# Linear attention before an MLP: the last k tile normalised in halves, and the sum over tokens taken ahead of the next q projection

## The chip, the cores and the metric

The kernel runs on one core of one Trainium2 chip. The metric is the time of one execution in microseconds (us), the median of three runs. The engines are PE (matmuls), DVE (vector), ACT (scalar), POOL (GpSimd) and SP (which issues DMAs here). Each works through its own list of instructions in order; semaphores tie the lists together.

## The reference

The block has two parts, each with a layer norm in front and a residual sum behind. The change touches only the first one, a linear attention with 32 heads of 16 features over 2048 tokens of 512 channels:

```python
q, k, v = split(layernorm(x) @ wqkv)
pq, pk = q @ w_phi, k @ w_phi                       # per head
phi_q = concat(softmax(pq), softmax(-pq))           # 32 features a head
phi_k = concat(softmax(pk), softmax(-pk))
kv  = einsum("bhsf,bhsd->bhfd", phi_k, v)
z   = einsum("bhsf->bhf", phi_k)                    # sum over all tokens
num = einsum("bhqf,bhfd->bhqd", phi_q, kv)
den = einsum("bhqf,bhf->bhq", phi_q, z)[..., None] + 1e-6
h = x + (num / den) @ wo
```

The second part, a token-mixing MLP with 1792 hidden units, follows on `layernorm(h)`.

## The kernel before, in words

The tokens are cut into 16 tiles of 128 (`NT = 16`). `w_phi` is folded into the q and k weights at the start, so that one projection gives the logits. Every projection of a tile is 12 matmuls of 128x512 (`mm3`, lines 68 to 70): the operands are split into a high and a low part, and three of the four products are summed for each of four chunks of channels.

For a k tile, `k_logits` takes the maximum and the minimum of each head's logits (`mx`, `mn`, lines 166 and 167) on DVE, subtracts them (`shift`, lines 160 and 164) and takes exponentials on ACT (line 186). `k_norm` then sums each head's exponentials on DVE (`sk`), inverts the sums, multiplies the tile `pk` by them on POOL (line 210) and adds it to `zacc` (lines 212 and 214). For the two last k tiles, 14 and 15, it is called with `z=False`, and the additions are written out elsewhere: that of tile 14 on POOL (line 485), that of tile 15 on DVE in two halves (line 493).

A v tile is projected by `v_proj` (`v_kv`, matmuls into `pv`); after every fourth one, `kv` multiplies four k tiles with their v tiles into `kvp`.

A q tile goes through the same logits. `q_mm` is its projection on PE, into one of two PSUM banks of the pool `ps_q` (the tile `pu`); `q_logits` returns three DVE steps (mx, mn and `shift`); `negate` forms the second half of the exponents on POOL (lines 174 and 175); `q_exp` takes the exponentials on ACT. Six q tiles (0 to 5) pass this way within the loop over the k tiles.

When the last k tile is added, a matmul of `ones` with `zacc` (line 501, two halves of 128x512, on PE) gives z in every partition, and ACT copies it to `zB` (line 502). Then follow for each q tile: `s_ez`, POOL's product of `eq` with `zB` (line 457, tile `ez`); `s_den`, five DVE steps from `ez` to the factors `w` (lines 466 to 470); `s_pq`, POOL's product of `eq` with `w` (line 473). The loop over q tiles (`it`) transposes the result on PE, multiplies it with kv and `wo`, adds x, and forms the second layer norm: `s_rstd` on POOL (line 610), `s_hn` on ACT and POOL (`hs`, line 64).

`wo_hi` and `wo_lo` split the weights `wo`, four pieces each: the high part on ACT (`woh`, line 442), the low part by subtraction on DVE (`wol`, line 445).

From line 94 to the end of this stage the order on PE, DVE, ACT and POOL is the order in which the code is written. `run` issues lists of steps; given more than one list, it takes a step of each in turn (`turns`).

Of the kernel before, what the change touches and what calls it, by code (L numbers as in the profile page):

```python
# [17 lines left out]
P = 128  # L18
S, D, H, DH, F = 2048, 512, 32, 16, 1792
NT = S // P  # L20
# [19 lines left out]
def block_kernel(ctx: ExitStack, tc: tile.TileContext, x, xT, wT, phic, wo, w1, b1, w2, b2,  # L40
                 kvmask, ident_in, out):
    nc = tc.nc
# [59 lines left out]
    zacc = wp.tile([P, NG, P], F32, name="zacc")  # L102
# [5 lines left out]
    X, XH, EQ, PK, VS, SQ, PS, W = {}, {}, {}, {}, {}, {}, {}, {}  # L108
# [23 lines left out]
    def proj(t, wh, wl, pool, name, by_part=False):  # L132
        o = pool.tile([P, D], F32, name=name, tag=name)
        if by_part:
            half, whole = [slice(0, D // 2), slice(D // 2, D)], slice(0, D)
            turn = [(0, wh, half[0]), (0, wh, half[1]), (1, wh, whole), (0, wl, half[0]), (0, wl, half[1])]
            for i, (a, w, cols) in enumerate(turn):
                for kt in range(KD):
                    nc.tensor.matmul(o[:, cols], X[t][:, a, kt, :], w[:, kt, cols], start=i == 0 and kt == 0,
                                     stop=i >= 3 and kt == KD - 1, skip_group_check=True)  # L140
            return o
        for kt in range(KD):
            mm3(o, X[t][:, 0, kt, :], X[t][:, 1, kt, :], wh[:, kt, :], wl[:, kt, :],
                kt == 0, kt == KD - 1)
        return o
# [6 lines left out]
    def logit_ops(src, e, pool):  # L152

        v = src.rearrange("p (j h d) -> p j h d", h=2, d=DH)
        ev = signs(e)
        mx = wk.tile([P, NPR, 2], F32, name="mx")
        mn = wk.tile([P, NPR, 2], F32, name="mn")

        def shift():
            nc.vector.tensor_sub(ev[:, :, 0], v, mx.unsqueeze(3).to_broadcast([P, NPR, 2, DH]))  # L160
            if pool:
                MN.append((ev, mx, mn))
            else:
                nc.vector.tensor_sub(ev[:, :, 1], mn.unsqueeze(3).to_broadcast([P, NPR, 2, DH]), v)  # L164

        return [lambda: nc.vector.tensor_reduce(mx, v, axis=AX.X, op=ALU.max),
                lambda: nc.vector.tensor_reduce(mn, v, axis=AX.X, op=ALU.min),
                shift]

    def negate():  # L170

        if MN:
            ev, mx, mn = MN.pop(0)
            nc.gpsimd.tensor_sub(mn, mn, mx)
            nc.gpsimd.tensor_sub(ev[:, :, 1], mn.unsqueeze(3).to_broadcast([P, NPR, 2, DH]), ev[:, :, 0])

    def turns(*lists):

        return [ops[i] for i in range(max(map(len, lists))) for ops in lists if i < len(ops)]

    def run(*lists):
        for op in turns(*lists):
            op()

    def exps(t, e):
        nc.scalar.activation(e, e, AF.Exp, scale=r1[:, t:t + 1])  # L186

    def heads(e):
        return e.rearrange("p g (a d) -> p (g a) d", d=DH)
# [16 lines left out]
    def k_norm(t, z=True):  # L206
        sk = wk.tile([P, 2 * H], F32, name="sk", bufs=2)
        nc.vector.reduce_sum(sk, heads(PK[t]), axis=AX.X)
        nc.vector.reciprocal(sk, sk)  # L209
        nc.gpsimd.tensor_mul(heads(PK[t]), heads(PK[t]), sk.unsqueeze(2).to_broadcast([P, 2 * H, DH]))  # L210
        if z and t == 0:
            nc.gpsimd.tensor_copy(zacc, PK[t])
        elif z:
            nc.gpsimd.tensor_add(zacc, zacc, PK[t])  # L214
# [17 lines left out]
    with tc.tile_pool(name="prep", bufs=1) as prep:  # L232
# [70 lines left out]
        with tc.manual_schedule(engines={ET.PE, ET.DVE, ET.Activation, ET.Pool}):  # L303
# [42 lines left out]
            stats_x(2)  # L346
            k3 = proj(3, wkh, wkl, ps_k, "pk_ps")
            k_norm(0)
            center(0, True)
            v_out(0, v0)  # L350
# [5 lines left out]
            fold(0, ps_q, "pu")  # L356
            fold(1, ps_q, "pu")
            k_norm(1)
            center(2, False)
            v_out(1, v1)  # L360
# [14 lines left out]
    def q_mm():  # L375
        if q["mm"] < NT:
            PS[q["mm"]] = proj(q["mm"], wqh, wql, ps_q, "pu")
            q["mm"] += 1

    def q_logits(lag):  # L380
        n = q["logits"]
        if n < min(NT, q["mm"] - lag + NT * (q["mm"] == NT)):
            EQ[n] = big.tile([P, NG, P], F32, name="eq", tag="big")
            q["logits"] += 1
            return logit_ops(PS[n], EQ[n], n >= len(Q_AT))
        return []

    def q_exp(lag):
        n = q["exp"]
        if n < min(NT, q["logits"] - len(MN) - lag):  # L390
            exps(n, EQ[n])
            q["exp"] += 1
# [8 lines left out]
    def v_kv():  # L401

        nonlocal v
        v_proj(v)
        if v % 4 == 0:
            for t in range(v - 4, v):
                kv(t)
        v += 1
# [4 lines left out]
    for t in range(3, NT - 1):  # L413
        if t + 2 < NT:
            raw = load_x(t + 2)
            load_h(t + 2)
        if t > 3:
            k_logits(t)
        if t > 3 and t not in V_NOT:
            v_kv()  # L420
        if t > 0:
            k_norm(t - 1)
        if t + 2 < NT:
            split_x(t + 2, raw)
            stats_x(t + 2)
        if t in Q_AT:
            q_mm()
            run(q_logits(0))
            q_exp(0)
            run(q_sums(1))  # L430
# [24 lines left out]
    def s_ez(t):  # L455
        EZ[t] = az.tile([P, NG, P], F32, name="ez")
        nc.gpsimd.tensor_mul(EZ[t], EQ[t], zB)  # L457

    def s_den(t):


        tz = az.tile([P, NPR, 2, 2], F32, name="tz")
        den = az.tile([P, NPR, 2], F32, name="den")
        W[t] = az.tile([P, NPR, 2, 2], F32, name="w", bufs=3)
        other = SQ[t][:, :, ::-1]
        return [lambda: nc.vector.reduce_sum(tz.rearrange("p g c h -> p (g c h)"), heads(EZ[t]), axis=AX.X),
                lambda: nc.vector.tensor_mul(tz, other, tz),
                lambda: nc.vector.reduce_sum(den, tz.rearrange("p g c h -> p g h c"), axis=AX.X),
                lambda: nc.vector.reciprocal(den, den),
                lambda: nc.vector.tensor_mul(W[t], other, den.unsqueeze(2).to_broadcast([P, NPR, 2, 2]))]  # L470

    def s_pq(t):
        nc.gpsimd.tensor_mul(heads(EQ[t]), heads(EQ[t]), W[t].rearrange("p g c h -> p (g c h)").unsqueeze(2).to_broadcast([P, 2 * H, DH]))  # L473
# [14 lines left out]
    for j in range(KD):  # L488
        wo_hi(j)
    v_kv()  # L490
    run(q_logits(0))
    for g in range(2):
        nc.vector.tensor_add(zacc[:, 4 * g:4 * g + 4, :], zacc[:, 4 * g:4 * g + 4, :], PK[NT - 1][:, 4 * g:4 * g + 4, :])
    for j in range(KD):
        wo_lo(j)
    negate()
    q_mm()
    zB = big.tile([P, NG, P], F32, name="zB", tag="big")
    for g in range(2):
        pz = ps_k.tile([P, 4, P], F32, name="pk_ps")  # L500
        nc.tensor.matmul(pz, ones, zacc[:, 4 * g:4 * g + 4, :], start=True, stop=True)
        nc.scalar.activation(zB[:, 4 * g:4 * g + 4, :], pz, AF.Identity, bias=eps2[:, 1:])  # L502
    q_exp(0)
    s_ez(0)
    s_ez(1)
    v_kv()
    run(s_den(0))
    run(q_logits(0))
    s_pq(0)
    negate()  # L510
    q_exp(0)
# [618 lines left out]
    for n, (sp, p) in enumerate(STEPS):  # L1130
        t = 2 * sp
# [131 lines left out]
```

## Time and profile before

| | |
|---|---|
| median of 3 runs | 517.39 us (517.29 to 517.85) |
| profiled execution | 516.99 us, span 515.2 us |
| PE busy | 509.3 us, 99% of the span |
| DVE, ACT, POOL busy | 445.9, 297.2, 244.6 us |
| granted PE clock | 1.00 |

The span reaches from the first to the last instruction. A row of the timeline has the start (us from the span's start), the duration, the engine, the line of the code, the operation, the output and inputs by the program's names with their sizes, and how often it stands there in a row; in square brackets stands the idle time of the engine ahead of it with what ended it. A row of the waits has who waited, for whom, the sum in us, how often, and the longest. A row of a group has the busy time and the mean duration in ns. The timeline's end of a matmul is modelled: matmuls overlap, and their starts are what counts.

### The profile page before, as it was taken

The numbers are of one execution on the slowest core, as the hardware profiler recorded it, in microseconds if no ns is written. First come the engines' busy times: TensorE is split into PE (matmuls) and PEld (weight loads), VectorE is DVE, ScalarE is ACT, GpSimd is POOL, SyncE is SP. The second block draws the span as 40 slices with busy tenths as digits, with TensorE's granted clock in tenths as the row PEclk, the third lists the DMA queues.
The fourth block names the chain that finished last, engine by engine and source line by source line (L and its number), as shares of the span: only waits on it lengthen the run. The fifth ranks groups of instructions, "written<-read, shape, count | busy, mean of one in ns | idle before, by whom it ended". The sixth has DMA issues, their size and how long they took to land.

```text
span 515.2 us, 9360 instructions
## 1 busy us (share of the span) xinstructions
PE 509.3 (99%) x3546; PEld 439.3 (85%) x3546; DVE 445.9 (87%) x765; ACT 297.2 (58%) x494; POOL 244.6 (47%) x188
## 2 busy tenths in 40 slices
PE   8999999999999999999999999999999999999997
PEld 8888888887877778777788899998888898899897
DVE  6793999986789998777796998989989899998985
ACT  6998954525245876668976643457753444444430
POOL 2579799984999999975343300000002212211220
PEclk9999999999999999999999999999999999999999
DMA  8844311000041324333322333374135688667833
GB/s 315 268 124 123 83 45 39 1 1 2 22 145 41 103 83 142 124 123 123 112 93 83 83 104 104 101 245 137 47 123 127 161 184 165 148 140 194 166 44 78
DMA packets 36300, 58.56 MB, mean 114 GB/s; under 512 B 3744, under 2 KB 19360, under 8 KB 36256
## 3 DMA queue, kind: packets, MB, share of 16 engines
q1 hardware_dynamic: 31648, 50.85, 31.5%
q0 software_dynamic: 4032, 6.42, 9.5%
q8 instruction: 28, 0.46, 0.4%
q10 hardware_dynamic: 576, 0.69, 0.4%
q14 instruction: 16, 0.13, 0.1%
HBM read 46.81 MB, written 11.14 MB: 112 GB/s over the span
## 4 chain that ended last, share of the span: by engine, by line
PE 94%; POOL 3%; ACT 1%; DVE 1%; issue 0%; POOLq 0%
PE py L1105 20%; PE pu L935 12%; PE pu L68 8%; PE pu L69 8%; PE pu L70 8%; PE py L1109 7%; PE pv L69 3%; PE pv L70 3%; PE pv L68 3%; PE pk_ps L68 3%; PE pk_ps L69 2%; PE pk_ps L70 2%; PE tn L547 2%; PE po L70 2%; PE po L69 2%; PE po L68 2%
## 5 line engine op out<-in xcount | busy, mean ns | idle before, releaser
L1181 POOL DMA_DIRECT2D out<-ot x7 | 6.2, 885 | 157.7 <-DVE ot L1177 157.7
L991 ACT ACTIVATE whi<-wraw 128x1792 fp32r<-128x1792 f32 x28 | 47.6, 1702 | 44.2 <-DVE wraw L858 26.6
L1001 DVE TENSOR_TENSOR wlo<-wraw,whi 128x1792 fp32r<-128x1792 f32 x28 | 56.6, 2020 | 4.9 <-PE py L1109 4.7
L1105 PE MATMUL py<-uf,whi 128*128 128x512 f32 x210 | 57.6, 393 | 0.0
L69 PE MATMUL pu<-hs,whi 128*128 128x512 f32 x128 | 50.3, 393 | 1.2 <-POOL hs L64 1.2
L68 PE MATMUL pu<-hs,whi 128*128 128x512 f32 x128 | 50.1, 399 | 0.0
L70 PE MATMUL pu<-hs,wlo 128*128 128x512 f32 x128 | 47.9, 390 | 0.0
L896 ACT ACTIVATE whi<-wraw 128x896 fp32r<-128x896 f32 x24 | 22.9, 955 | 31.2 <-PE pu L935 26.2
L457 POOL TENSOR_TENSOR ez<-eq,zB 128x1024 f32<-128x1024 f32 x16 | 38.3, 2396 | 4.5 <-ACT zB L502 4.5
L1105 PEld LDWEIGHTS py<-uf,whi 128*128 128x128 f32 x210 | 35.8, 189 | 4.3
L1105 PEld LDWEIGHTS py<-uf,wlo 128*128 128x128 f32 x210 | 33.1, 190 | 4.6
L935 PE MATMUL pu<-ht,whi 128*128 128x256 f32 x192 | 35.6, 283 | 0.0
L1105 PE MATMUL py<-uf,wlo 128*128 128x256 f32 x210 | 34.9, 280 | 0.0
L210 POOL TENSOR_TENSOR pk<-pk,sk 128x1024 f32<-128x1024 f32 x16 | 31.0, 1941 | 6.3 <-DVE sk L209 6.3
L64 POOL TENSOR_TENSOR hs<-hb,hs 128x512 fp32r<-128x512 f32 x16 | 22.3, 1393 | 24.4 <-ACT hs L63 24.3
L549 ACT ACTIVATE pht<-tn 128x512 f32<-128x512 f32 x32 | 17.4, 596 | 28.6 <-PE tn L547 28.4
L473 POOL TENSOR_TENSOR eq<-eq,w 128x1024 f32<-128x1024 f32 x16 | 32.2, 2013 | 0.8 <-DVE w L470 0.8
L214 POOL TENSOR_TENSOR zacc<-zacc,pk 128x1024 f32<-128x1024 f32 x13 | 31.2, 2402 | 0.6
L186 ACT ACTIVATE pk<-pk,r 128x1024 f32<-128x1024 f32 x16 | 18.3, 1146 | 21.1 <-DVE pk L164 21.1
L68 PEld LDWEIGHTS pu<-hs,whi 128*128 128x128 f32 x128 | 24.0, 188 | 7.1 <-issue 2.5
L935 PEld LDWEIGHTS pu<-ht,whi 128*128 128x128 f32 x192 | 30.0, 192 | 0.0
L69 PEld LDWEIGHTS pu<-hs,whi 128*128 128x128 f32 x128 | 24.1, 188 | 6.6 <-POOL hs L64 2.1
(208 smaller groups left out, 1606.6 us busy)
## 6 DMA issues: line engine op xcount, KB each, us to landing
wraw<-in_w SPq DMA_DIRECT2D x28, 512.0 KB, 4.2
wraw<-in_w SPq DMA_DIRECT2D x48, 256.0 KB, 2.8
xraw<-in_xT SPq DMA_DIRECT2D x16, 256.0 KB, 3.0
xh<-in_x SPq DMA_DIRECT2D x16, 256.0 KB, 2.7
h<-in_x SPq DMA_DIRECT2D x16, 256.0 KB, 2.8
out<-h SPq DMA_DIRECT2D x14, 256.0 KB, 2.7
out<-ot POOLq DMA_DIRECT2D x14, 256.0 KB, 4.9
wraw<-in_wT SPq DMA_DIRECT2D x12, 256.0 KB, 5.1
```

The lines of the kernel that those rows point to most:

```text
L68: nc.tensor.matmul(o, ah, bh, start=first, stop=False)
L69: nc.tensor.matmul(o, ah, bl, start=False, stop=False)
L70: nc.tensor.matmul(o, al, bh, start=False, stop=last)
L210: nc.gpsimd.tensor_mul(heads(PK[t]), heads(PK[t]), sk.unsqueeze(2).to_broadcast([P, 2 * H, DH]))
L214: nc.gpsimd.tensor_add(zacc, zacc, PK[t])
L457: nc.gpsimd.tensor_mul(EZ[t], EQ[t], zB)
L473: nc.gpsimd.tensor_mul(heads(EQ[t]), heads(EQ[t]), W[t].rearrange("p g c h -> p (g c h)").unsqueeze(2).to_broadcast([P, 2 * H, DH]))
L935: nc.tensor.matmul(ACC[p][bk][:, half], WS[p, i][x][:, a], hb[b][y], start=i == 0 and half == 0 and k == 0, stop=i == NT // 2 - 1 and k == ...
L991: nc.scalar.activation(WH[g], RAW[g], AF.Copy)
L1001: nc.vector.tensor_sub(wl_, RAW[g], WH[g])
L1105: nc.tensor.matmul(o, w, u, start=p == 0 and not low, stop=p == NP - 1, skip_group_check=True)
L1109: nc.tensor.matmul(bank[bk][:, half], AW[sp, p][x][:, a], UB[p, b][:, y], start=p == 0 and half == 0 and i == 0, stop=p == NP - 1 and i == ...
```

## The change

The multiplication of the last k tile by its inverted sums becomes two instructions, each for half of the columns. DVE's additions to `zacc` are issued alternately with the logits of q tile 6 instead of behind them. The matmuls with `ones` and the copies to `zB` stand ahead of the next `q_mm` (q tile 7) instead of behind it. Further on, the first of the three logit steps of q tile 7 stands ahead of `s_den(0)`, and the other two stay behind it.

```diff
         nc.vector.reciprocal(sk, sk)
-        nc.gpsimd.tensor_mul(heads(PK[t]), heads(PK[t]), sk.unsqueeze(2).to_broadcast([P, 2 * H, DH]))
+        n = 1 if z or t < NT - 1 else 2
+        for part in range(n):
+            a = slice(2 * H // n * part, 2 * H // n * (part + 1))
+            nc.gpsimd.tensor_mul(heads(PK[t])[:, a], heads(PK[t])[:, a],
+                                 sk[:, a].unsqueeze(2).to_broadcast([P, 2 * H // n, DH]))
...
     v_kv()
-    run(q_logits(0))
-    for g in range(2):
-        nc.vector.tensor_add(zacc[:, 4 * g:4 * g + 4, :], zacc[:, 4 * g:4 * g + 4, :], PK[NT - 1][:, 4 * g:4 * g + 4, :])
+    run([lambda g=g: nc.vector.tensor_add(zacc[:, 4 * g:4 * g + 4, :], zacc[:, 4 * g:4 * g + 4, :],
+                                          PK[NT - 1][:, 4 * g:4 * g + 4, :]) for g in range(2)], q_logits(0))
     for j in range(KD):
         wo_lo(j)
     negate()
-    q_mm()
     zB = big.tile([P, NG, P], F32, name="zB", tag="big")
     for g in range(2):
         pz = ps_k.tile([P, 4, P], F32, name="pk_ps")
         nc.tensor.matmul(pz, ones, zacc[:, 4 * g:4 * g + 4, :], start=True, stop=True)
         nc.scalar.activation(zB[:, 4 * g:4 * g + 4, :], pz, AF.Identity, bias=eps2[:, 1:])
+    q_mm()
     q_exp(0)
     s_ez(0)
     s_ez(1)
     v_kv()
-    run(s_den(0))
-    run(q_logits(0))
+    ops = q_logits(0)
+    run(ops[:1], s_den(0))
+    run(ops[1:])
     s_pq(0)
```

On DVE, this is the stretch from the last inverted sums of a k tile to the first factors `w`, before the change (`pu_1473` holds the logits of q tile 6, `pu_1523` those of q tile 7, `pk_1370` is k tile 15):

```order
L209 RECIPROCAL sk_1486<-sk_1486 128x64
L166 TENSOR_REDUCE mx_1510<-pu_1473 128x32
L167 TENSOR_REDUCE mn_1511<-pu_1473 128x32
L160 TENSOR_TENSOR eq_1509<-pu_1473,mx_1510 128x16x32
L493 TENSOR_TENSOR zacc_109<-zacc_109,pk_1370 128x512 x2
L445 TENSOR_TENSOR wol_1383<-wor_1384,woh_1382 128x512 x4
L466 TENSOR_REDUCE tz_1563<-ez_1544 128x64
L467 TENSOR_TENSOR tz_1563<-smq_83,tz_1563 128x64
L468 TENSOR_REDUCE den_1564<-tz_1563 128x32
L469 RECIPROCAL den_1564<-den_1564 128x32
L470 TENSOR_TENSOR w_1565<-smq_83,den_1564 128x64
L166 TENSOR_REDUCE mx_1572<-pu_1523 128x32
```

The same stretch of DVE after the change, where `pu_1531` holds the logits of q tile 7:

```order
L209 RECIPROCAL sk_1486<-sk_1486 128x64
L495 TENSOR_TENSOR zacc_109<-zacc_109,pk_1370 128x512
L166 TENSOR_REDUCE mx_1511<-pu_1473 128x32
L495 TENSOR_TENSOR zacc_109<-zacc_109,pk_1370 128x512
L167 TENSOR_REDUCE mn_1512<-pu_1473 128x32
L160 TENSOR_TENSOR eq_1510<-pu_1473,mx_1511 128x16x32
L449 TENSOR_TENSOR wol_1383<-wor_1384,woh_1382 128x512 x4
L166 TENSOR_REDUCE mx_1565<-pu_1531 128x32
L470 TENSOR_REDUCE tz_1567<-ez_1545 128x64
L471 TENSOR_TENSOR tz_1567<-smq_83,tz_1567 128x64
L472 TENSOR_REDUCE den_1568<-tz_1567 128x32
L473 RECIPROCAL den_1568<-den_1568 128x32
```

Both additions now stand ahead of mn and `shift` of q tile 6, and the maximum of q tile 7 stands between the four `wol` and `tz`. All else keeps its order; the line numbers of the second half are 2 to 4 higher.

On POOL, the rows from the addition of k tile 14 to the first two `ez` and the first `s_pq`, before the change:

```order
L485 TENSOR_TENSOR zacc_109<-zacc_109,pk_1323 128x1024
L210 TENSOR_TENSOR pk_1370<-pk_1370,sk_1486 128x1024
L174 TENSOR_TENSOR mn_1511<-mn_1511,mx_1510 128x32
L175 TENSOR_TENSOR eq_1509<-mn_1511,eq_1509 128x16x32
L457 TENSOR_TENSOR ez_1544<-eq_584,zB_1536 128x1024
L457 TENSOR_TENSOR ez_1546<-eq_779,zB_1536 128x1024
L473 TENSOR_TENSOR eq_584<-eq_584,w_1565 128x1024
```

And the same rows of POOL after it:

```order
L489 TENSOR_TENSOR zacc_109<-zacc_109,pk_1323 128x1024
L213 TENSOR_TENSOR pk_1370<-pk_1370,sk_1486 128x512 x2
L174 TENSOR_TENSOR mn_1512<-mn_1512,mx_1511 128x32
L175 TENSOR_TENSOR eq_1510<-mn_1512,eq_1510 128x16x32
L461 TENSOR_TENSOR ez_1545<-eq_584,zB_1524 128x1024
L461 TENSOR_TENSOR ez_1547<-eq_779,zB_1524 128x1024
L477 TENSOR_TENSOR eq_584<-eq_584,w_1569 128x1024
```

Only the multiplication has changed, from one instruction to two of half the width.

## The prediction

> **What bounds the kernel now.** I read the page first: busy time by engine and the chain of work that ended last.
>
> ```profile
> PE 509.3 (99%) x3546; PEld 439.3 (85%) x3546; DVE 445.9 (87%) x765; ACT 297.2 (58%) x494; POOL 244.6 (47%) x188
> PE 94%; POOL 3%; ACT 1%; DVE 1%; issue 0%; POOLq 0%
> ```
>
> PE is busy for 509.3 of 515.2 us, and the chain is PE for 94%. Work moved on another engine is worth only what it does to a moment in which PE stands still. So the second view is PE's own waits, and the longest of them in the timeline:
>
> ```profile
> PE pu L69 <- POOL hs L64: 1.2, 1, 1.2
> 187.50 0.50 PE L69 MATMUL pu<-hs,whi 128*128 128x512 f32 x1 [1.15 <-POOL hs L64]
> ```
>
> That is the one wait of PE behind POOL, more than 60 us after the place of the change. At the change itself, the waits between 118 and 139 us name no PE wait worth the name. They do show that two other engines stand still:
>
> ```profile
> POOL ez L457 <- ACT zB L502: 4.5, 1, 4.5
> DVE tz L466 <- POOL ez L457: 4.0, 1, 4.0
> ```
>
> POOL waits 4.5 us for zB, then DVE waits 4.0 us for POOL's first `ez`. The change brings zB forward. The timeline of PE there (start, us) gives the reason for these waits and PE's dates:
>
> ```profile
> 122.32 0.39 PE L70 MATMUL pv<-wvh,xs 128*128 128x512 f32 x1
> 122.55 0.39 PE L68 MATMUL pu<-wqh,xs 128*128 128x512 f32 x1
> 125.28 1.88 PE L501 MATMUL pk_ps<-zacc,ones 128*128 128x512 f32 x4
> 129.72 0.39 PE L68 MATMUL pu<-wqh,xs 128*128 128x512 f32 x1
> 134.94 0.39 PE L70 MATMUL pv<-wvh,xs 128*128 128x512 f32 x1
> 135.16 0.39 PE L68 MATMUL pu<-wqh,xs 128*128 128x512 f32 x1
> ```
>
> Three q projections begin at 122.55 (q tile 7), 129.72 (8) and 135.16 (9). The pool `ps_q` has two banks, so tile 9 writes where tile 7 stood, and must wait until DVE's last reader of tile 7 is done.
>
> **The change part by part.** First DVE and POOL as they are:
>
> ```profile
> 119.03 1.93 POOL L210 TENSOR_TENSOR pk<-pk,sk 128x1024 f32<-128x1024 f32 x1 [1.08 <-DVE sk L209]
> 122.09 1.35 POOL L175 TENSOR_TENSOR eq<-mn,eq 128x512 f32<-128x512 f32 x1 [0.43 <-DVE eq L160]
> 127.96 4.75 POOL L457 TENSOR_TENSOR ez<-eq,zB 128x1024 f32<-128x1024 f32 x2 [4.52 <-ACT zB L502]
> 132.92 1.94 POOL L473 TENSOR_TENSOR eq<-eq,w 128x1024 f32<-128x1024 f32 x1 [0.21 <-DVE w L470]
> 134.82 0.26 POOL L174 TENSOR_TENSOR mn<-mn,mx 128x32 f32<-128x32 f32 x1
> 135.16 1.06 POOL L175 TENSOR_TENSOR eq<-mn,eq 128x512 f32<-128x512 f32 x1
> 136.17 2.40 POOL L457 TENSOR_TENSOR ez<-eq,zB 128x1024 f32<-128x1024 f32 x1
> 138.53 1.94 POOL L473 TENSOR_TENSOR eq<-eq,w 128x1024 f32<-128x1024 f32 x1
> ...
> 120.03 0.69 DVE L166 TENSOR_REDUCE mx<-pu 128x32 f32<-128x512 f32 x1 [1.17 <-PE pu L70]
> 120.64 0.68 DVE L167 TENSOR_REDUCE mn<-pu 128x32 f32<-128x512 f32 x1
> 121.24 0.68 DVE L160 TENSOR_TENSOR eq<-pu,mx 128x512 f32<-128x512 f32 x1
> 121.83 2.15 DVE L493 TENSOR_TENSOR zacc<-zacc,pk 128x512 f32<-128x512 f32 x2
> 123.91 2.48 DVE L445 TENSOR_TENSOR wol<-wor,woh 128x512 fp32r<-128x512 f32 x4
> 130.40 1.22 DVE L466 TENSOR_REDUCE tz<-ez 128x64 f32<-128x1024 f32 x1 [4.00 <-POOL ez L457]
> 132.55 0.23 DVE L470 TENSOR_TENSOR w<-smq,den 128x64 f32<-128x64 f32 x1
> 132.69 0.68 DVE L166 TENSOR_REDUCE mx<-pu 128x32 f32<-128x512 f32 x1
> 133.89 0.68 DVE L160 TENSOR_TENSOR eq<-pu,mx 128x512 f32<-128x512 f32 x1
> ```
>
> Two things are to be seen. DVE instructions follow each other every 0.60 us. And two instructions lasted longer than their like: POOL's L175 took 1.35 at 122.09 and 1.06 at 135.16; the two additions of L493 took 2.15 together, though two in a row end after 0.60 + 0.68 = 1.28. They collided: an addition with both operands in SBUF and a POOL instruction do not run at once. The first addition (121.83 to 122.51) held L175 back until 122.38, about 0.14 before its recorded end; L175 ended at 123.44 and the second addition at 123.98, 0.54 later. What happens where POOL has more instructions queued is to be read near 185 us, where a subtraction of the same kind as `wol` met two POOL instructions:
>
> ```profile
> 183.39 2.38 POOL L457 TENSOR_TENSOR ez<-eq,zB 128x1024 f32<-128x1024 f32 x1
> 185.73 1.72 POOL L64 TENSOR_TENSOR hs<-hb,hs 128x512 fp32r<-128x512 f32 x1
> ...
> 184.40 1.92 DVE L664 TENSOR_TENSOR wlo<-wraw,whi 128x512 fp32r<-128x512 f32 x1
> ```
>
> The subtraction waited until `ez` ended at 185.77 and ended 0.55 later; only then did POOL's next instruction run, ending at 187.45. So they take turns: the one that waits goes next.
>
> *The halved multiplication.* One instruction becomes two. Its price: the whole takes 1.94, the same form at 128x512 (L175, free) 1.06, at 128x32 0.26; so a half is 1.06. Bounds: 0.97, half of the whole, below which it cannot lie since the elements stay the same; and 1.39, the mean of POOL's dearest instruction of that size:
>
> ```profile
> L64 POOL TENSOR_TENSOR hs<-hb,hs 128x512 fp32r<-128x512 f32 x16 | 22.3, 1393 | 24.4 <-ACT hs L63 24.3
> ```
>
> L175 is nearest, as it also spreads its second operand. The halves stand at 119.03 to 120.09 and 120.05 to 121.11 (POOL starts the next 0.04 before a recorded end: 138.53 against 136.17 + 2.40).
>
> *The additions between the logits.* The first may start at 120.13, but the second half is then running: it ends at 121.11 + 0.55 = 121.66. Then at 0.60 each: mx 121.58, second addition 122.18 to 122.86, mn 122.78, the subtraction of `shift` 123.38 to 124.06, `wol` from 123.98. Before, `wol` began at 123.91. DVE gains nothing; the collision has only moved from L175 to the second half.
>
> *The product ahead of the q projection.* PE reaches it at 122.55 and its second half about 0.9 later (half of 1.88). The additions end at 121.66 and 122.86: 0.9 and 0.6 in time, so this costs 0. PE's work is the same, only in another order; nothing is moved on ACT, SP or any DMA queue. The copies to zB follow the product:
>
> ```profile
> 126.34 0.69 ACT L502 ACTIVATE zB<-pk_ps,eps 128x512 f32<-128x512 f32 x1 [2.84 <-PE pk_ps L501]
> 127.20 0.69 ACT L502 ACTIVATE zB<-pk_ps,eps 128x512 f32<-128x512 f32 x1 [0.17 <-PE pk_ps L501]
> ```
>
> They end 2.61 after the product's start, so at 125.16 instead of 127.89.
>
> *What that lets loose.* Before, the four `wol` subtractions had POOL idle beside them: 2.48 in all. Now `shift` ends at 124.06, L175 asks 0.17 later as before (121.92 and 122.09), at 124.23, and POOL has both `ez` ready behind it. Taking turns: first `wol` to 124.66, L175 124.52 to 125.58, second `wol` to 126.13, first `ez` to 128.38 (126.0 + 2.39), third `wol` to 128.93, second `ez` to 131.18, fourth `wol` to 131.73. The `wol` end 5.3 later than at 126.39. Queued behind them are q tile 7's mx at 131.65 and `s_den(0)` from 132.25. As before, `w` starts 2.15 after `tz`: 134.40 (132.55 before), mn 0.14 later, then `shift` 135.14 to 135.82. Before, it ended at 134.57, 0.59 ahead of PE's third q projection at 135.16. Now PE waits until about 135.87: **0.7 us**.
>
> *POOL after that.* L473 starts 0.37 after `w`, at 134.77, 1.85 late. Does that reach PE's wait at 187.50? The waits of POOL between 126 and 190 us, and the timeline:
>
> ```profile
> POOL eq L473 <- DVE w L470: 0.8, 3, 0.4
> POOL r L610 <- ACT ve L605: 0.9, 1, 0.9
> 160.64 2.38 POOL L457 TENSOR_TENSOR ez<-eq,zB 128x1024 f32<-128x1024 f32 x1
> 163.97 0.55 POOL L610 TENSOR_TENSOR r<-ve,mhalf 128x1 f32<-128x1 f32 x1 [0.94 <-ACT ve L605]
> ```
>
> Two of the three waits for `w`, 0.6 together, lie behind 134 us and swallow part; 1.25 are left. At 163.02 POOL waited 0.94 for ACT, whose work there follows PE's and comes 0.7 later: room for 1.64. So from 163.97 on everything is 0.7 late, no more, and the wait at 187.50 stays 1.15. For the same reason a lead of POOL would not survive 163.97.
>
> *Sum:* the profiled execution took 516.99 (span 515.2 and 1.79 around it); 517.7 now. The median of the runs shown, 517.39, lies 0.4 above that execution, so 517.39 + 0.7 = **518.1**. With a half at 0.97 the wait is 0.5, since two halves stand in the path.
>
> The Trainium skill (SBUF — State Buffer, section Who interferes with whom) states that a VectorE instruction with two SBUF inputs and a GpSimd instruction exclude each other for the whole instruction, and that whoever issues first wins: a rule against this change. The trace agrees that one waits, but not for the whole: the waiting addition ended 0.54 after L175, not 0.68.
>
> **The rivals.**
>
> *Dear halves (slower).* Every 0.1 more for a half adds 0.2 to PE's wait. It decides from 1.23 on, where the wait passes 1.03, which is 0.2% and about what a measurement of this kernel can tell from no change. At 1.39 the wait is 1.36: 518.8. For it: instructions of this size reach 1.39. Against: the row of 1.06. 0.17.
>
> *POOL keeps the port for its queue.* Then L175 and both `ez` run to 130.28, three `wol` end at 130.83, 131.43 and 132.03, and `shift` 0.3 later than forecast: 1.0, thus 518.4, on the border. Against: 184.40. 0.11.
>
> *Whole instructions shut each other out.* Seven hand-overs on the path, each 0.14 dearer: 1.0 more, 519.1. Against: the 2.15 of L493. This is what the skill's sentence would make of it. 0.04.
>
> *No collision with `wol`* (another order of arrival): DVE is done at 126.4, `s_den(0)` starts near 127.7, PE never waits: 517.4. Speaking for it: DVE had all this room before. 0.10.
>
> *Faster:* POOL's lead of up to 2.7 us (127.89 against 125.16) lives to 187.50 and takes its 1.15 away: 516.2. Against: the wait at 163.97 eats any lead. 0.08.
>
> **How the numbers follow.** The forecast has 0.50, and by itself reaches from 517.8 to 518.5. Faster by over 0.2%: 0.08, the last rival. Slower by over 0.2% (above 518.4): 0.17 + 0.04, half of the second rival, and 0.03 of the forecast's upper end: 0.30. The rest, 0.62, is within 0.2%. The range goes from the case without a collision less 0.3 for the scatter of medians to near the dearest: 517.1 to 519.0.
>
> **What would show it.** Right: halves near 1.06; the first L493 about 1.5 long; zB ended near 125.2; three `wol` of over 1.5; `shift` of tile 7 ending near 135.8; a new PE wait of about 0.7 near 135 us, released by DVE; L610 still waiting for ACT. Wrong: `wol` of 0.68 each, a PE wait in front of the product, or a changed wait near 188 us.

## The result, and the profile after

| | before | changed |
|---|---|---|
| median of 9 runs | 517.39 us (517.03 to 518.24) | 518.48 us (518.00 to 518.90) |
| profiled execution | 516.99 us, span 515.2 | 518.80 us, span 517.0 |

The ratio is 1.0019 (95% interval 1.0011 to 1.0027): the changed kernel is slower by about 1.0 us (0.6 to 1.4). Its median lies 0.4 above the forecast of 518.1, inside the forecast range of 517.1 to 519.0.

The page of the changed kernel, busy time and the chain that ended last:

```profile
PE 509.4 (99%) x3546; PEld 438.8 (85%) x3546; DVE 451.4 (87%) x765; ACT 297.5 (58%) x494; POOL 245.8 (48%) x189
PE 87%; DVE 5%; POOL 3%; ACT 2%; DMA 1%; issue 1%; SPq 0%; DVEq 0%; POOLq 0%; ACTq 0%
```

PE does the same work as before. DVE is busy 5.5 us longer, none of it with more instructions, and stands in the chain with 5% instead of 1%. Two rows of PE's own waits in the changed kernel:

```profile
PE pu L286 <- DVE wraw L276: 0.7, 1, 0.7
PE pu L68 <- DVE eq L160: 0.6, 1, 0.6
```

The last row is the wait that was forecast: a q projection behind `shift`. The row above it belongs to the start of the kernel, which the change does not touch. It must come off before the two executions are compared. The first 20 us of before, then of the changed kernel (window, then for each engine busy time and instructions, then granted clock, DMA share and GB/s):

```profile
0.00:20.00 20.00, 18.64 (x111) 16.51 (x111) 15.89 (x34) 15.44 (x33) 5.67 (x9) 1.00 0.92 319
```

```profile
0.00:20.00 20.00, 17.61 (x109) 15.91 (x110) 15.13 (x32) 14.63 (x31) 5.70 (x9) 1.00 0.91 316
```

In the second one PE did 1.0 us less in that time, and the last inverted sums ahead of the change start at 119.15 instead of 118.31. So this execution was 0.84 us late when it came to the change. That is scatter of the start and not the change: among the executions below, the same instruction starts anywhere from 118.14 to 118.77, and at 118.72 in `hs_ahead_678`, whose code up to there is that of the kernel before. I take 0.84 off each date.

DVE in the changed kernel (timeline, as in the prediction):

```profile
119.15 0.55 DVE L209 RECIPROCAL sk<-sk 128x64 f32<-128x64 f32 x1
120.97 1.53 DVE L495 TENSOR_TENSOR zacc<-zacc,pk 128x512 f32<-128x512 f32 x1 [1.26 <-POOL pk L213]
...
124.82 7.75 DVE L449 TENSOR_TENSOR wol<-wor,woh 128x512 fp32r<-128x512 f32 x4
...
129.69 2.88 DVE L449 TENSOR_TENSOR wol<-wor,woh 128x512 fp32r<-128x512 f32 x1
...
135.97 0.68 DVE L160 TENSOR_TENSOR eq<-pu,mx 128x512 f32<-128x512 f32 x1
```

The four `wol` take 7.75 us where they took 2.48. They are not slower in themselves: they stand between POOL's instructions. (The row of 2.88 is the last of the four, as a narrower window shows it alone; so is the row of 2.84 below, the second `ez`.) The same stretch of POOL and ACT:

```profile
119.87 2.08 POOL L213 TENSOR_TENSOR pk<-pk,sk 128x512 f32<-128x512 f32 x2 [1.09 <-DVE sk L209]
...
125.07 1.34 POOL L175 TENSOR_TENSOR eq<-mn,eq 128x512 f32<-128x512 f32 x1 [0.43 <-DVE eq L160]
126.38 5.64 POOL L461 TENSOR_TENSOR ez<-eq,zB 128x1024 f32<-128x1024 f32 x2
...
129.18 2.84 POOL L461 TENSOR_TENSOR ez<-eq,zB 128x1024 f32<-128x1024 f32 x1
...
135.60 1.94 POOL L477 TENSOR_TENSOR eq<-eq,w 128x1024 f32<-128x1024 f32 x1 [3.58 <-DVE w L474]
...
165.73 0.55 POOL L614 TENSOR_TENSOR r<-ve,mhalf 128x1 f32<-128x1 f32 x1 [0.62 <-ACT ve L609]
...
125.30 0.69 ACT L504 ACTIVATE zB<-pk_ps,eps 128x512 f32<-128x512 f32 x1 [0.17 <-PE pk_ps L503]
```

POOL no longer waits 4.52 us for zB: its `ez` runs at 126.38, beside `wol`. The two `ez` take 5.64 instead of 4.75. The last `wol` waits until the second `ez` ends at 132.02 and ends itself at 132.57, 0.55 later. What this does to PE:

```profile
123.39 1.88 PE L503 MATMUL pk_ps<-zacc,ones 128*128 128x512 f32 x4
...
135.76 0.39 PE L70 MATMUL pv<-wvh,xs 128*128 128x512 f32 x1
136.80 0.47 PE L68 MATMUL pu<-wqh,xs 128*128 128x512 f32 x1 [0.64 <-DVE eq L160]
...
139.41 0.39 PE L70 MATMUL pu<-wqh,xs 128*128 128x512 f32 x1
...
189.28 0.50 PE L69 MATMUL pu<-hs,whi 128*128 128x512 f32 x1 [1.18 <-POOL hs L64]
```

No idle time stands in front of the product with ones. At the third q projection PE starts 1.04 us after the matmul ahead (136.80 - 135.76), where it was 0.22: 0.82 lost. The eleven matmuls that follow need 2.61 to the last start (139.41 - 136.80). Before, they needed 2.50 (from 135.16):

```profile
137.66 0.39 PE L70 MATMUL pu<-wqh,xs 128*128 128x512 f32 x1
```

That is 0.11 more. The wait for `hs` is 1.18, against 1.15. So the spans differ by 0.84 + 0.82 + 0.11 = 1.77, and 1.8 was measured; without the late start it is 0.93, and the ratio of the medians gives 1.0.

### The profile page after: what moved, and what is told of

The parts are those of the page before. It is cut to its first block, busy times and chain, and to the rows that moved or that the text cites. A ratio compares the mean times of both kernels' runs of the same rounds, so it can differ in the third digit from the quotient of the medians.

```text
span 517.0 us, 9361 instructions
## 1 busy us (share of the span) xinstructions
PE 509.4 (99%) x3546; PEld 438.8 (85%) x3546; DVE 451.4 (87%) x765; ACT 297.5 (58%) x494; POOL 245.8 (48%) x189
## 4 chain that ended last, share of the span: by engine, by line
PE 87%; DVE 5%; POOL 3%; ACT 2%; DMA 1%; issue 1%; SPq 0%; DVEq 0%; POOLq 0%; ACTq 0%
PE py L1109 20%; PE pu L939 12%; PE pu L68 8%; PE pu L69 7%; PE pu L70 7%; PE py L1113 7%; PE tn L551 2%; PE po L70 2%; PE pk_ps L68 2%; PE pk_ps L69 2%; PE pk_ps L70 2%; PE po L69 2%; PE po L68 2%; PE pv L69 2%; PE pv L70 2%; PE pv L68 2%
## 5 line engine op out<-in xcount | busy, mean ns | idle before, releaser
L213 POOL TENSOR_TENSOR pk<-pk,sk 128x1024 f32<-128x1024 f32 (+1 forms) x17 | 31.2, 1839 | 6.6 <-DVE sk L209 6.6
L477 POOL TENSOR_TENSOR eq<-eq,w 128x1024 f32<-128x1024 f32 x16 | 32.2, 2014 | 3.6 <-DVE w L474 3.6
```

What stands on the lines that cost most here:

```text
L213: nc.gpsimd.tensor_mul(heads(PK[t])[:, a], heads(PK[t])[:, a], sk[:, a].unsqueeze(2).to_broadcast([P, 2 * H // n, DH]))
```

## The experiments

**The collision with wol.** The theory is that the whole loss comes from `wol` taking turns with POOL, and POOL's `ez` being there so early through zB. Two kernels take the collision away and leave all the rest of the change. In the first, the second operand of `wol` comes from PSUM. For that it subtracts the logits of q tile 6 in place of `woh`, so its `wol` is not the low part of `wo` and only its time is of use:

```diff
-        nc.vector.tensor_sub(wol[:, j], WO[j], woh[:, j])
+        nc.vector.tensor_sub(wol[:, j], WO[j], PS[q["logits"] - 1])
```

> The changed kernel, but the four wol subtractions read their second operand from PSUM (the logits of q tile 6) instead of SBUF, so they no longer share a port with POOL; wol has other values, everything else is computed as before. Theory (wol takes turns with POOL): the four last 0.68 each and end near 126.4 by the clock of the kernel before, shift of q tile 7 ends near 131.5 or earlier, the PE wait of 0.6 to 0.8 at the third q projection is gone, the wait near 188 stays 1.1 to 1.2; ratio to before 1.000 (within 0.0005). Rival 1 (the halved multiplication and the additions cost it): still 1.001 to 1.002. Rival 2 (the product ahead of the q projection costs PE itself): still 1.001 to 1.002.

Its time was 517.29 us, ratio to before 1.0000 (0.9991 to 1.0009). The timeline of DVE and POOL:

```profile
124.28 2.47 DVE L449 TENSOR_TENSOR wol<-wor,pu 128x512 fp32r<-128x512 f32 x4
130.99 0.68 DVE L160 TENSOR_TENSOR eq<-pu,mx 128x512 f32<-128x512 f32 x1
...
125.55 4.77 POOL L461 TENSOR_TENSOR ez<-eq,zB 128x1024 f32<-128x1024 f32 x2
```

`wol` is back at 2.47 and both `ez` at 4.77, although they overlap in time; `shift` of q tile 7 starts at 130.99, and PE's wait for it is gone. POOL now is ahead of the kernel before: its first L477 starts at 130.62 instead of 132.92. That lead of 2.3 us brought nothing at the end. It was gone long before the wait for `hs`:

```profile
144.66 1.94 POOL L477 TENSOR_TENSOR eq<-eq,w 128x1024 f32<-128x1024 f32 x1 [2.80 <-DVE w L474]
```

Before, POOL waited 0.19 for `w` at this place (144.36). DVE could not make `w` sooner, since it waited 4.58 for PE's `kvp` itself (1.39 before). By 160.93 POOL's `ez` starts where it did before (160.64), but for the 0.3 us by which this execution came late to the change.

The second leaves both operands in SBUF and makes one instruction of four:

```diff
-    for j in range(KD):
-        wo_lo(j)
+    nc.vector.tensor_sub(wol, wor, woh)
```

> The changed kernel, but wol is one subtraction of 128x2048 instead of four of 128x512; both operands stay in SBUF. Theory (each hand-over of the port costs DVE one POOL instruction): one instruction of about 2.3 us starts before POOL's half of the exponents asks and holds it back, DVE is free near 126.4, there is no PE wait at the third q projection; ratio 1.000. Rival (sharing a port is costly as such, by the elements that are read): DVE and POOL together need as long as before and the ratio stays 1.001 to 1.002.

Its time was 517.19 us, 0.9995 (0.9986 to 1.0004). DVE and POOL:

```profile
124.39 2.27 DVE L497 TENSOR_TENSOR wol<-wor,woh 128x2048 fp32r<-128x2048 f32 x1
...
124.64 2.95 POOL L175 TENSOR_TENSOR eq<-mn,eq 128x512 f32<-128x512 f32 x1 [0.44 <-DVE eq L160]
```

The one instruction was there first and ran through. POOL's L175 waited for it (2.95 instead of 1.06), once, and PE waits for nothing there: `shift` of q tile 7 starts at 132.87. So it is the number of turns that costs, not the subtraction itself.

**The parts of the change.** The first kernel puts `q_mm` back ahead of the product, and with it the old order of `s_den(0)` and the logits:

```diff
     negate()
+    q_mm()
...
-    q_mm()
     q_exp(0)
...
-    ops = q_logits(0)
-    run(ops[:1], s_den(0))
-    run(ops[1:])
+    run(s_den(0))
+    run(q_logits(0))
```

> Only the halved multiplication and the additions between the logits; the product with ones stands behind the q projection and the logits behind the denominators, as before. Theory: zB is ready at the same time as before (product start + 2.6), POOL's ez meet no wol, no new PE wait: ratio 1.000. Rival 1 (the halves and the additions are what costs): 1.001 to 1.002.

517.26 us, 0.9997 (0.9988 to 1.0006). The timeline:

```profile
123.99 3.35 DVE L449 TENSOR_TENSOR wol<-wor,woh 128x512 fp32r<-128x512 f32 x4
...
127.96 4.77 POOL L461 TENSOR_TENSOR ez<-eq,zB 128x1024 f32<-128x1024 f32 x2 [2.38 <-ACT zB L505]
```

With the late zB, `wol` meets only L175 (3.35), and `ez` starts at 127.96 as before. Halves and alternating additions alone neither cost nor gain anything that can be measured.

The second kernel is the one before with nothing but `q_mm` moved behind the product and its copies:

```diff
     negate()
-    q_mm()
...
         nc.scalar.activation(zB[:, 4 * g:4 * g + 4, :], pz, AF.Identity, bias=eps2[:, 1:])
+    q_mm()
     q_exp(0)
```

> Only the product ahead of the q projection; the multiplication whole, the additions behind the logits, the denominators ahead of the logits, as before. Theory: the second addition ends at 123.98 as before, but PE now reaches the second half of the product near 123.45, so PE waits about 0.6 in front of it; DVE has only the last wol left when ez starts, so no wait at the third q projection: ratio 1.0012 from another place. Rival 2 (the moved product costs PE as such): 1.002 or more, with the wait at the third q projection too.

518.08 us, 1.0016 (1.0007 to 1.0025). Its PE waits in front of the second half of the product, and not at the q projection:

```profile
122.90 1.10 PE L500 MATMUL pk_ps<-zacc,ones 128*128 128x512 f32 x2
124.36 1.10 PE L500 MATMUL pk_ps<-zacc,ones 128*128 128x512 f32 x2 [0.36 <-DVE zacc L493]
...
122.07 2.14 DVE L493 TENSOR_TENSOR zacc<-zacc,pk 128x512 f32<-128x512 f32 x2
124.14 2.49 DVE L445 TENSOR_TENSOR wol<-wor,woh 128x512 fp32r<-128x512 f32 x4
...
126.26 4.99 POOL L457 TENSOR_TENSOR ez<-eq,zB 128x1024 f32<-128x1024 f32 x2 [2.60 <-ACT zB L501]
```

From the start of the first half to the end of the second it takes 2.56 us (124.36 + 1.10 - 122.90); undisturbed it takes 1.88, so 0.68 is lost there. The second addition ended at 124.21, since it had to let L175 go first. In exchange zB comes later than in the full change, and only the last `wol` is still running when `ez` arrives at 126.26. There `ez` is the one that waits (4.99 for the two instead of 4.77), and `wol` keeps its 2.49. The two parts are thus not additive: the halves and the earlier additions do remove the wait that the moved product would have, and by that bring zB into the stretch of `wol`.

**The logits around the factors.** Two kernels move the maximum of q tile 7. With all three logit steps ahead of `s_den(0)`, the buffer that PE waits for should come free early:

```diff
-    ops = q_logits(0)
-    run(ops[:1], s_den(0))
-    run(ops[1:])
+    run(q_logits(0))
+    run(s_den(0))
```

> The changed kernel with all three logit steps of q tile 7 ahead of the denominators of q tile 0. Theory: shift of tile 7 ends 2.4 us earlier, so no PE wait at the third q projection; but w of tile 0 comes 1.2 us later than in the changed kernel, POOL stays later, and the exponential of q tile 7 on ACT, which waits for POOL, holds back the copy of the last v tile behind it, for which PE waits in front of kvp near 140 us, about 1.6 us: ratio 1.003. Rival (the late shift of tile 7 is all that counts): 1.000.

519.04 us, 1.0031 (1.0019 to 1.0043): by its median slower than the change itself, though the two intervals overlap. Its `shift`, two rows of ACT and one of POOL, then a row of PE's waits:

```profile
132.89 0.67 DVE L160 TENSOR_TENSOR eq<-pu,mx 128x512 f32<-128x512 f32 x1
...
139.31 1.15 ACT L186 ACTIVATE eq<-eq,r 128x1024 f32<-128x1024 f32 x1 [8.61 <-POOL eq L175]
140.37 0.67 ACT L201 ACTIVATE vs<-pv,r 128x512 f32<-128x512 f32 x1
...
135.99 1.94 POOL L477 TENSOR_TENSOR eq<-eq,w 128x1024 f32<-128x1024 f32 x1 [4.78 <-DVE w L474]
```

```profile
PE kvp L226 <- ACT vs L201: 1.6, 1, 1.6
```

`shift` starts at 132.89 instead of 135.13 (135.97 with the 0.84 off), and PE's wait for it is gone. But `w` is later, so POOL's L477 (135.99 instead of 134.76), L175 behind it and the exponential that needs L175 are later too; ACT's copy `vs` stands behind that exponential, and PE waits 1.6 for `vs`. One wait is traded for a longer one.

The other kernel puts the maximum back behind `s_den(0)`, as it was before the change:

```diff
-    ops = q_logits(0)
-    run(ops[:1], s_den(0))
-    run(ops[1:])
+    run(s_den(0))
+    run(q_logits(0))
```

> The changed kernel with the maximum of q tile 7 back behind the denominators of q tile 0. Theory: the three logit steps and the five denominator steps need the same time in either order, so shift of tile 7 ends at the same time and the PE wait at the third q projection stays 0.6 to 0.8: ratio 1.001 to 1.002, as for the changed kernel. Rival (the maximum ahead of tz makes it late): 1.000 to 1.0005.

518.46 us, 1.0021 (1.0012 to 1.0030), as the full change. PE there:

```profile
135.40 0.39 PE L70 MATMUL pv<-wvh,xs 128*128 128x512 f32 x1
136.43 0.47 PE L68 MATMUL pu<-wqh,xs 128*128 128x512 f32 x1 [0.65 <-DVE eq L160]
...
139.04 0.39 PE L70 MATMUL pu<-wqh,xs 128*128 128x512 f32 x1
```

The starts are 1.03 apart, and the last of the twelve matmuls starts 2.61 after the first (139.04 - 136.43), as in the full change. (This execution came 0.46 late to the change: its last inverted sums start at 118.77.) The moved maximum costs and gains nothing that can be measured.

**The wait at 187 us.** The last rival had the lead of POOL pay at PE's one old wait, for `hs`. `wol_from_psum` had a lead and no gain, so that wait should depend on POOL's order there: `hs` stands behind an `ez` that nobody needs yet. The kernel before with that `ez` moved behind `s_hn` in iteration 6:

```diff
-        if it + 3 < NT:
+        late = it == 6
+        if it + 3 < NT and not late:
             s_ez(it + 3)
...
         if it >= 4 and even:
             s_hn(it - 4)
+        if it + 3 < NT and late:
+            s_ez(it + 3)
```

> The kernel before, with POOL's subtraction for hs ahead of its ez in iteration 6 of the loop over q tiles. Theory (the wait at 187.50 is POOL's own order): hs ends 2.4 us earlier, the wait of 1.15 goes, and 0.3 to 0.5 comes back at a later place since POOL has no less to do: ratio 0.9985 to 0.999. Rival (POOL is full there, so the wait only moves): 1.000.

516.93 us, 0.9990 (0.9981 to 0.9998). PE's waits have a new row, and the timeline has its reason:

```profile
PE pu L70 <- DVE wlo L664: 0.6, 1, 0.6
```

```profile
189.80 3.48 DVE L664 TENSOR_TENSOR wlo<-wraw,whi 128x512 fp32r<-128x512 f32 x2
...
189.84 2.89 POOL L457 TENSOR_TENSOR ez<-eq,zB 128x1024 f32<-128x1024 f32 x1
```

The wait for `hs` is gone, and half of the gain goes to the next collision of the same kind, between the subtraction `wlo` and an `ez`. Doing the same to the changed kernel shows whether the two places depend on each other (its diff is that of `hs_ahead_before`):

> The changed kernel with hs ahead of ez in iteration 6. Theory: its two waits are independent, 0.8 stays at the third q projection, and the gain is that of the kernel before with the same edit: ratio near 1.0006 (1.0016 less 0.001). Rival (the waits after 187 depend on the moment at which wlo and ez meet, as with wol in one): 1.001 or more.

517.63 us, 1.0007 (0.9998 to 1.0015), 0.83 less than `mx_behind`, which was timed beside it. Its PE has both new waits and no old one:

```profile
PE pu L68 <- DVE eq L160: 0.6, 1, 0.6
PE pu L70 <- DVE wlo L668: 0.6, 1, 0.6
```

Within the intervals each place costs what it costs alone. I then joined the cure for `wol` with this edit (the diffs of `wol_in_one` and `hs_ahead_before`, on the changed kernel):

> The changed kernel with wol in one subtraction and hs ahead of ez in iteration 6. Theory: both waits are gone and the two edits do not meet: the ratio of the kernel before with hs ahead, 0.9985 to 0.999. Rival: POOL, ahead by up to 2.5 us until 164 us, also keeps something of that lead: below 0.9985.

This one missed: 518.12 us (517.61 to 519.47), 1.0017 (1.0006 to 1.0028). DVE and POOL, then three windows of PE (window, busy time and matmuls, granted clock, DMA share, GB/s):

```profile
190.25 4.37 DVE L667 TENSOR_TENSOR wlo<-wraw,whi 128x512 fp32r<-128x512 f32 x2 [0.21 <-issue]
...
190.01 2.40 POOL L461 TENSOR_TENSOR ez<-eq,zB 128x1024 f32<-128x1024 f32 x1
192.36 1.72 POOL L64 TENSOR_TENSOR hs<-hb,hs 128x512 fp32r<-128x512 f32 x1
```

```profile
190.00:194.60 4.60, 2.97 (x40) 1.00 0.10 19
194.60:196.00 1.40, 1.32 (x5) 0.90 0.90 328
196.00:198.00 2.00, 2.00 (x6) 0.50 0.70 198
```

Here `ez` began 0.24 ahead of `wlo`, where it had been 0.04 behind. DVE stood idle for 0.21 in front of `wlo`. What it waited for no view names (the row says "issue"); but this idle time of 0.20 to 0.23 stands there in the three kernels with `wol` in one piece and in none of the others, so the two edits do meet. `wlo` waited for `ez` and then, between its two pieces, for `hs`; PE waited 1.7 us, and after that wait the granted clock fell to 0.50. The three of nine runs whose mean clock was 0.996 or 0.997 took 519.3 to 519.5, the six others 517.6 to 518.5.

If this meeting is the cause, moving the `ez` behind `hs` in iterations 7 and 8 as well takes it off `wlo`:

```diff
-        late = it == 6
+        late = it in (6, 7, 8)
...
-        if it + 3 < NT and late:
+        if it + 3 < NT and late and even:
             s_ez(it + 3)
...
         if it >= 4 and not even:
             s_hn(it - 4)
+        if it + 3 < NT and late and not even:
+            s_ez(it + 3)
```

On the kernel before:

> The kernel before with hs ahead of ez in iterations 6, 7 and 8. Theory: the 1.15 at 187.50 goes as with iteration 6 alone, and the wait of 0.6 for wlo near 193 goes too, since hs no longer stands between ez and the second wlo: ratio 0.998 to 0.9985. Rival (an ez that comes later holds up its denominators): 0.999 or above.

516.46 us, 0.9981 (0.9972 to 0.9990); neither `hs` nor `wlo` keeps PE waiting. `wlo` now runs while POOL waits for ACT, with `ez` behind `hs`:

```profile
190.21 1.28 DVE L664 TENSOR_TENSOR wlo<-wraw,whi 128x512 fp32r<-128x512 f32 x2
...
191.64 1.28 POOL L64 TENSOR_TENSOR hs<-hb,hs 128x512 fp32r<-128x512 f32 x1 [1.35 <-ACT hs L63]
192.89 2.40 POOL L457 TENSOR_TENSOR ez<-eq,zB 128x1024 f32<-128x1024 f32 x1
```

And on the changed kernel together with the one-piece `wol`:

> The changed kernel with wol in one subtraction and hs ahead of ez in iterations 6, 7 and 8. Theory: as the kernel before with hs ahead in these iterations, 0.998 to 0.9985, and without the scatter up to 519.4 of the version with iteration 6 alone, since the second wlo meets no hs. Rival (PE without a pause is granted less clock): a stretch at half the clock in the profile, ratio above 1.000.

516.33 us (516.20 to 517.10), 0.9985 (0.9976 to 0.9993). It has no wait of PE for `hs`, `wlo` or `shift` and is faster than both kernels. Beside `hs_ahead_678` it is the same within the intervals, so the gain is the order at 187 us; the change, cured of its collision, still adds nothing.

## Why the prediction was right

*The halves* took 2.08 together; two of 1.06 with 0.04 of overlap were forecast. *The first addition* lasted 1.53 and ended at 121.66 with the 0.84 taken off, as forecast. *The product* stood without a wait, as forecast, and `product_alone` shows that this was earned by the earlier additions. *zB* ended at 125.99, so 125.15 against 125.16.

*Taking turns*, the step on which the sign rested, came out whole: `wol` lasted 7.75, which is what 123.98 to 131.73 makes, the last of the four 2.88, and `shift` of q tile 7 ended at 136.65, so 135.81 against 135.82. The Trainium skill (SBUF — State Buffer, section Who interferes with whom) has the two engines exclude each other for a whole instruction, the first to issue winning. The trace agrees on who goes first, but not on the whole instruction: a `wol` that waited ended 0.55 behind POOL and not 0.68. The stretch has six hand-overs, and at 0.14 more for each it would have taken about 8.6 by estimate. This refutes the rival of *whole instructions*. That `wol_from_psum` and `wol_in_one` lose PE's wait and the whole loss shows that this collision was the cause.

*The rest of POOL* behaved as worked out: L614 still waited 0.62 for ACT, and the wait for `hs` stayed at 1.18. That a lead does not survive was tested apart from the change: 2.3 us of it in `wol_from_psum` were worth nothing. The prediction was right in this but named the wrong place. The lead went at 144.66, in POOL's wait for `w`, and the wait for ACT at 164 us, which it held to be what eats a lead, was 0.95 there as in the kernel before (0.94).

Two terms were too small. From the end of `shift` to PE's start I took 0.05, for which I had no row; it was 0.15 (136.65 to 136.80, and again in `mx_behind`). And I had the matmuls behind the wait run at their usual pace; they took 0.11 more. With both, the 0.7 becomes 0.9, which is what the trace shows and near the 1.0 of the medians. The rest of the difference is within the interval.

Of the rivals, *dear halves* and *no collision* are refuted by the two rows of 2.08 and 7.75. *POOL keeps the port* would have had both `ez` end ahead of the second `wol`; they took 5.64 with `wol` between them. *Faster* is refuted by the wait for `hs`, which stayed. The outcome, 0.19%, lies just inside the bound of 0.2%, with its interval on both sides of it.

## What to carry to other kernels

A result that comes sooner starts its consumer sooner, so look at what runs at that moment on an engine that cannot run beside the consumer; here four subtractions that had had POOL idle beside them became the chain that PE waits for. Where small two-input instructions must share a stretch with POOL, make them one, or read one operand from PSUM, where the algorithm has it there: here both brought the whole loss back. An instruction that nobody needs yet should stand behind the one that PE waits for, and here the first swap of that kind uncovered the next.

## What the hardware showed that I had not expected

Turns are decided by very little: 0.24 us between `ez` and `wlo` instead of -0.04 made PE's wait 1.7 instead of 0.6. After the wait at the third q projection PE's next eleven matmuls took 0.11 longer, at a granted clock of 1.00, in both executions looked at. After the wait of 1.7 us in `wol_one_hs_ahead` the clock was at 0.50 in the profiled execution. The Trainium skill (TensorE: Matmul & The Clock Gate, section Why this matters for your kernels) warns of gaps of more than about 3 us; here the clock fell after 1.7, and the mean clocks of 0.996 to 0.997 suggest the same in two other runs. The length of the wait alone does not decide it: in `logits_first` PE waited 1.63, and in the 6.8 us after that the clock stayed at 1.00:

```profile
141.20:148.00 6.80, 6.80 (x65) 1.00 0.89 301
```

What does decide it was not tried.
